# Weight loads queued behind a small transfer out of a gathered tile, and separate buffers for the copies of narrow tiles

## The chip, the cores and the metric

The kernel runs on one core of one Trainium2 chip. The metric is the device time of one execution in microseconds (us). The core has TensorE (PE in the profile), VectorE (DVE), ScalarE (ACT), GpSimd (POOL) and SyncE (SP), each with a queue of its own that it works through in order, and 16 DMA engines that all transfers share.

## The reference

```python
kv  = einsum('bhsd,bhse->bhde', k, v)           # batch 8, heads 8, seq 576, head_dim 64
a   = einsum('bhsd,bhde->bhse', q, kv)
a   = a / sqrt(mean(a*a, -1) + 1e-6) * g_norm
x   = a.transpose(0, 2, 1, 3).reshape(4608, 512)
e   = argmax(x @ w_gate); gate_w = softmax prob of e      # 8 experts
h   = relu(disp[e] @ w1[e])                      # 512 -> 1024
y   = h @ w2[e]                                  # 1024 -> 512
out = gate_w * y, back in token order (rows beyond an expert's capacity stay 0)
```

All inputs and outputs are float32.

## The kernel before, in words

The first part, up to about 166 us, computes the attention batch by batch, writes the rows (each with its normalization factor and gate) to a DRAM tensor `x_dram`, and builds a table that says which token stands in which slot of which expert. One expert, picked early, is the first; its first 384 rows (`EARLY`) are already under way in that part.

The second part goes through the eight experts in turn, with a fixed number of rows each (`BUDGET`: 704, 672, 640, 624, 592, 576, 560, 512), cut into tiles of 128 rows and a remainder. For an expert:

- **Rows.** GpSimd gathers a tile of rows from `x_dram` with an indirect DMA (`Rows.fetch`, line 439) into one of four buffers `xg`. VectorE or GpSimd multiplies by the normalization factor (`norm`, line 447). For the remaining rows 384 to 704 of the first expert (`rows`, line 1173; three tiles, of 128, 128 and 64 rows) TensorE transposes the result (line 459), and ScalarE and VectorE copy it into a high and a low float16 half `xs` (lines 677 and 467). For the other experts (`rows_beside`, line 1589) the two halves are made first and a DMA transpose on SP's queue turns them (line 482).
- **Weights.** SP loads `w1` and `w2` of the next expert in quarters of 512 KB into `raw1` and `raw2` (`load_weight`, line 327). VectorE takes the maximum of every eighth (line 343), one more instruction joins them (`a`, line 351), TensorE carries that across partitions (lines 356 and 363), VectorE makes a scale (lines 367 to 372), ScalarE writes the high half (line 377) and VectorE the low half (line 383). `weights` (line 1538) sets this up; its argument `after` names operations behind which the loads are planned. For the second expert that is the list `sent` that `rows` returns: the issues of the first expert's three gathers.
- **Products.** TensorE computes the first product in eight column blocks (line 531) into two PSUM buffers; ScalarE takes the high half of the rectified result (line 536), VectorE the low half (line 539). The second product (line 577) writes a PSUM bank per tile; ScalarE scales it into a buffer `ysb` (line 602) and GpSimd scatters it to `out` (line 607). A tile of at most 112 rows (`NARROW`; six experts have one) is computed the other way round (line 586); VectorE copies it to `yt` (`keep`, line 592), TensorE transposes it back (line 597), and then it goes to `ysb`. `yt` and `ysb` share one ring of three buffers.

The order on every engine is written by a planner (`Plan`, line 96) when the program is built: a list scheduler in which every operation has a duration, dependences, a key for its priority, and rings that model buffers. SP issues and DMA transfers are operations of it too ("S" and "D"). The order it finds is emitted engine by engine; on the chip the engines run through it and wait for one another by semaphores. A changed dependence or ring can therefore move other instructions in any engine's order.

Of the kernel before, what the change touches and what calls it, by code (L numbers as in the profile page):

```python
# [12 lines left out]
F32 = mybir.dt.float32  # L13
# [67 lines left out]
class Ring:  # L81
# [3 lines left out]
    def new(self):  # L85
        self.holds.append(Hold(self.holds[-self.n] if len(self.holds) >= self.n else None))
        return self.holds[-1]
# [8 lines left out]
class Plan:  # L96
# [5 lines left out]
    def op(self, ways, fn, deps=(), key=0.0, takes=(), uses=(), late=0.0):  # L102

        ways = [ways] if isinstance(ways[0], str) else list(ways)
        o = Op(ways, fn, [d for d in deps if d is not None], list(takes), key, late)
        for h in takes + uses if isinstance(takes, tuple) and isinstance(uses, tuple) else list(takes) + list(uses):
            h.users.append(o)
        self.ops.append(o)
        return o
# [56 lines left out]
def attention_moe_kernel(  # L166
# [12 lines left out]
    nc = tc.nc  # L179
    NB, H, S, D = q.shape  # L180
    N, DM = out.shape
    E = w_gate.shape[1]
    F = w1.shape[2]
    P = 128
# [67 lines left out]
    warm = cst.tile([1, 1], F32, name="warm")  # L252
# [21 lines left out]
    kv_bds = []  # L274
    for i in range(2):
        t = cst.tile([P, H, 2, XW], F32, name=f"kv_bd{i}")
        nc.gpsimd.memset(t, 0.0)
        kv_bds.append(t)


    mv_all = cst.tile([P, NT], F32, name="mv_all")
# [134 lines left out]
    def spans(s0, s1):  # L416

        cuts = [s0] + list(range((s0 // P + 1) * P, s1, P)) + [s1]
        return [(a, b - a, NHI if a % P else a // P) for a, b in zip(cuts, cuts[1:])]

    class Rows:


        def __init__(self, pool, gidx, s0, s1, size, bufs=3, rows=N, raw=None):
            self.pool, self.gidx, self.s0, self.bufs, self.rows, self.raw = pool, gidx, s0, bufs, rows, raw or pool
            self.tiles = spans(s0, s1)
            apart = "" if raw is None else f"_{s0}"
            self.xs = pool.tile([P, 2, KD, size], F16, name="xs" + apart)
            self.gt = pool.tile([P, NHI], F32, name="gt" + apart)
            self.xg, self.xm, self.pair = {}, {}, {}  # L430
# [122 lines left out]
    class Gemm2:  # L553
# [34 lines left out]

        def keep(self, i, yp):
            n = self.tiles[i][1]  # L590
            self.yt = self.pool.tile([P, DM], F32, tag="ysb", name="yt", bufs=self.bufs)
            nc.vector.tensor_copy(self.yt[:, 0:KD * n], yp[:, 0:KD * n])

        def turn(self, i, yp):
# [74 lines left out]
    op = plan.op  # L669
# [3 lines left out]
    new = lambda n: rings[n].new()  # L673

    def copy(e, out_, in_):
        if e == "A":
            nc.scalar.copy(out_, in_)
        else:
            nc.vector.tensor_copy(out_, in_)
# [41 lines left out]
    def kv_products(b, ts):  # L721
# [52 lines left out]

        o = op(("T", 0.31), turn, cut, key + 1, (a2,), (ks,))
        o = op([("A", 0.29), ("V", 0.34)], keep, [o], key + 1, (kt,), (a2,))
        o = op(("T", 0.42), gates, [o, ready], key + 1, (a3,), (kt,))
        done = [spread(u, f) for u in range(2) for f in range(2)]
# [12 lines left out]
    def unit(b, n, ts, kv, ready, oh):  # L791
# [18 lines left out]

        o = op(("T", 0.11 * m), turn, [qd], key - 1.2, (qp,), (qh,))
        kept = op([("A", 0.06 + 0.105 * m), ("V", 0.07 + 0.133 * m)], keep, [o], key - 1, (qt,), (qp,))
        done = []
        for w in range(2 if two else 1):
# [358 lines left out]
    def rows(gidx, s0, s1, n, slots_, key, low, pool, raw, bank, hold=None, size=None):  # L1173

        st, hold = {}, hold or Hold(None)
        fetched, gates, highs, lows = [], [], [], []
        landed = [w for ws in writes for w in ws]

        def fetch(e, i):
            if i == 0:  # L1180
                st["rows"] = Rows(pool, gidx()[0], s0, s1, size or s1 - s0, 3 if raw else 4, n, raw)
            st["rows"].fetch(i)

        for i in range(len(spans(s0, s1))):
            xg, xm, xp = new("xg"), new("xm"), new("x")
            o = op(("P", 1.05), lambda e, i=i: fetch(e, i), slots_ + landed + fetched[:1], key, (hold, xg))
            fetched.append(o)
            o = op(("D", 0.85), None, [o], key, (), (xg,))
            a = op([("V", 0.61), ("P", 1.05)], lambda e, i=i: st["rows"].norm(i, nc.vector if e == "V" else nc.gpsimd), [o],
                   low, (xm,), (xg,))  # L1190
            gates.append(op(("V", 0.07), lambda e, i=i: st["rows"].gate(i), [o], low, (), (xg, hold)))

            def turn(e, i=i, xp=xp):
                xp.t = bank()
                st["rows"].turn(i, xp.t)

            a = op(("T", 0.44), turn, [a], low, (xp,), (xm,))
            a = op([("A", 0.48), ("V", 0.61)],
                   lambda e, i=i, xp=xp: st["rows"].high(i, xp.t, lambda out_, in_: copy(e, out_, in_)), [a], low, (),
                   (xp, hold))  # L1200
            highs.append(a)
            lows.append(op(("V", 0.61), lambda e, i=i, xp=xp: st["rows"].low(i, xp.t), [a], low, (), (xp, hold)))
        return st, hold, fetched, (gates, highs, lows)

    def second(r, st, hh, hl, w2, scaled, hid, w_hold, sl_hold, s0, s1, bank, tiles=range(NHI), key=None):

        key = KEY * r if key is None else key
        urgent = key - KEY
        for i, (_, m, _) in enumerate(spans(s0, s1)):
            if i not in tiles:  # L1210
                continue
            yp, o = new(bank[0]), None
            k = key + 5 + 0.1 * i
            if m > NARROW:
                for c in range(0, 3 * KF, 4):

                    def product(e, i=i, c=c, yp=yp):
                        if c == 0:
                            yp.t = bank[1]()
                        st["g2"].products(i, yp.t, c, c + 4)  # L1220

                    js = range(c % KF, c % KF + 4)
                    after = [(hl if c >= 2 * KF else hh)[j] for j in js] + [scaled, o]
                    after += [w2[KF <= c < 2 * KF][j] for j in js] if w2 else []
                    o = op(("T", 0.86), product, after, k, (yp,), (hid, w_hold))
            else:
                yt = new("ysb")

                def product(e, i=i, yp=yp):
                    yp.t = bank[1]()  # L1230
                    st["g2"].turned_products(i, yp.t)

                o = op(("T", m / 25 + (0.25 if m > 50 else 0.5 if m > 40 else 1.1)), product, hh + hl + [scaled] + [x[j] for x in w2 or () for j in range(KF)], k, (yp,),
                       (hid, w_hold))
                o = op(("V", 0.07 + 4 * m / 960), lambda e, i=i, yp=yp: st["g2"].keep(i, yp.t), [o], urgent, (yt,), (yp,))
                yp = new(bank[0])

                def turn(e, i=i, yp=yp):
                    yp.t = bank[1]()
                    st["g2"].turn(i, yp.t)  # L1240

                o = op(("T", 0.4), turn, [o], key + KEY + 0.05, (yp,), (yt,))
            yh = new("ysb")

            def out_(e, i=i, yp=yp, yh=yh):
                yh.t = st["g2"].out(i, yp.t)

            o = op(("A", 0.58), out_, [o], urgent, (yh,), (yp,))
            o = op(("P", 1.05), lambda e, i=i, yh=yh: st["g2"].write(i, yh.t), [o], key, (), (yh, sl_hold))
            o = op(("D", 0.73), None, [o], key, (), (yh,))  # L1250
        return o
# [222 lines left out]
    def rest(last, n_i, e_tab, t_tab, keyc, zrow_i):  # L1474
        n_any = nc.values_load(n_i[0:1, 1:2], min_val=0, max_val=MAXT + 2)
        with tc.If(n_any > 0):
# [17 lines left out]
            with tc.For_i(0, n_t) as i:  # L1494
# [29 lines left out]
                for f in steps:  # L1524
# [3 lines left out]
    plan = Plan(plan.free)  # L1528
    op = plan.op
    rings.update({n: Ring(m) for n, m in (("h", 2), ("y", 2), ("x", 2), ("xs", 2), ("xg", 4), ("xm", 2), ("pair", 2),  # L1530
                                          ("ysb", 3), ("hid", 1), ("slots", 3))})
    for i in range(2):
        rings.update({f"w{i}_{s}": Ring(1) for s in range(2)} | {f"e{i}": Ring(2)})
        rings.update({f"raw{i}_{p}": Ring(1) for p in range(4)})
# [89 lines left out]
    def products(r, x, xh, xl, gates, xs_hold, si, sl_hold, sets, zs, w_holds, s0, s1):  # L1624
# [29 lines left out]
        def scales(e):  # L1654
# [3 lines left out]
        scaled = op(("V", 1.2), scales, hh[:1] + gates + [o for _, o, _ in zs], urgent, (),  # L1658
                    (xs_hold, *[x for _, _, x in zs]))
        o = second(r, st, hh, hl, sets and sets[1], scaled, hid, w_holds[1], sl_hold, s0, s1, y_bank)  # L1660
        if r == REST_AFTER:
            early["later"] = scaled
# [10 lines left out]
    o = op(("S", 0.01), moved, [early["scaled"]], -9 * KEY, (), tuple(ews))  # L1673
# [6 lines left out]
    for r in range(E):  # L1680
        products(r, *args)
        key = KEY * r
        if r + 1 < E:
            before = [] if r > 1 else sent
            st, xs_hold, sl, gates, turned, sent, asked = rows_beside(r + 1, key + ROWS)
# [3 lines left out]
        else:  # L1689
            steps, o = plan_rest(), early["later"]  # L1690
            for _ in range(68):
                o = op(("V", 0.2), lambda e: next(steps, None), [o], key + 1)
# [36 lines left out]
```

## Time and profile before

| | |
|---|---|
| median of 3 runs | 579.97 us (577.83 to 583.57) |
| the profiled execution's own time | 578.9 us |
| its span, first to last instruction | 577.1 us |
| mean granted TensorE clock | 0.968 of full speed |
| busy, share of the span | PE 91%, DVE 66%, ACT 43%, POOL 38% |
| HBM read and written | 73.13 MB and 20.61 MB |

Times in the rows count from the first instruction of the span. A row of the timeline says when a run of like instructions began, how long it took, how many it were, and in square brackets how long the engine had been idle before and what it waited for. The recorded ends of TensorE instructions are modelled; the starts are not.

### The profile page before, as it was taken

Reading aid. Unit: us, or ns where it says so; the run is one execution under the profiler, and the core shown is the slowest. Engines: PE = TensorE matmul, PEld = TensorE weight load, DVE = VectorE, ACT = ScalarE, POOL = GpSimd, SP = SyncE. Lnnn points to the kernel's source line nnn. Section 1 sums busy time; section 2 is a strip of 40 time slices with the busy share of each in tenths; the row PEclk is TensorE's granted clock in tenths of the full one; section 3 lists DMA queues with packets and bytes.
Section 4 is the critical chain, followed back from the end, with each engine's and each line's share of the span. In section 5 each row is a group of like instructions: output and inputs, shape, how many; then the busy total and the mean of one; then the engine's idle time right before and its main releaser. Section 6 shows DMA issues by size and latency. Waiting matters only on the chain.

```text
span 577.1 us, 12423 instructions
## 1 busy us (share of the span) xinstructions
PE 525.8 (91%) x4727; PEld 346.3 (60%) x4727; DVE 378.3 (66%) x1007; ACT 250.9 (43%) x496; POOL 218.1 (38%) x290
## 2 busy tenths in 40 slices
PE   4969697896997979998999999999999999999995
PEld 4868686683544646643774476477557648845442
DVE  4357679989976978999899186638629615721200
ACT  2737475875412536471825253362525445211210
POOL 3002332455334578556343632464263271011011
PEclk9979899986998999999999999999999999999998
DMA  8997999744249659595965572756365251011001
GB/s 277 374 347 242 352 370 378 233 160 154 94 134 351 152 139 336 110 314 186 222 224 155 132 196 78 218 111 225 113 163 195 77 100 50 2 37 38 0 31 38
DMA packets 78021, 102.61 MB, mean 178 GB/s; under 512 B 43222, under 2 KB 51414, under 8 KB 76932
## 3 DMA queue, kind: packets, MB, share of 16 engines
q1 hardware_dynamic: 69600, 70.43, 41.5%
q0 software_dynamic: 7776, 31.30, 15.6%
q8 instruction: 39, 0.64, 0.5%
q14 instruction: 26, 0.21, 0.1%
q10 hardware_dynamic: 580, 0.02, 0.1%
HBM read 73.13 MB, written 20.61 MB: 162 GB/s over the span
## 4 chain that ended last, share of the span: by engine, by line
PE 25%; issue 15%; DMA 5%; DVE 2%; POOL 2%; ACT 1%; POOLq 0%; DVEq 0%; ACTq 0%
PE yp L577 12%; PE hp L531 12%; DMA out_dram<-ysb,si 5%; PE yp L586 1%; DVE w2l L383 1%; POOL xg L439 1%; DVE hl L539 1%; POOL xm L447 0%; ACT w1h L377 0%; ACT w2h L377 0%; POOLq L1664 0%; POOL pair L477 0%; POOL out_dram L607 0%; PE pt_max L356 0%; PE pt_max L363 0%
## 5 line engine op out<-in xcount | busy, mean ns | idle before, releaser
L531 PE MATMUL hp<-xs,w1h 128*128 128x320 f16 (+6 forms) x896 | 134.1, 301 | 0.4 <-DVE hl L539 0.3
L531 PEld LDWEIGHTS <-w1h 128*128 128x128 f16 x960 | 94.0, 99 | 43.2 <-issue 5.9
L607 POOL DMA_INDIRECT out_dram<-ysb,si x41 | 43.0, 1048 | 143.0 <-ACT ysb L602 108.6
L577 PEld LDWEIGHTS <-hh 128*128 128x128 f16 x560 | 54.5, 98 | 65.4 <-issue 2.3
L536 ACT ACTIVATE hh<-hp 128x320 f16<-128x320 f32 (+7 forms) x64 | 40.8, 637 | 110.8 <-PE hp L531 108.2
L343 DVE TENSOR_REDUCE am<-raw 128x1 f32<-128x512 f32 x120 | 75.5, 675 | 4.3 <-DMA raw<-in_moe_w_dram 4.2
L531 PE MATMUL hp<-xs,w1l 128*128 128x320 f16 (+6 forms) x448 | 71.5, 300 | 0.0
L477 POOL TENSOR_TENSOR pair<-xm,pair 128x512 f16<-128x512 f32 (+5 forms) x35 | 45.1, 1290 | 64.8 <-ACT pair L473 60.0
L539 DVE SCALAR_TENSOR_TENSOR hl<-hp,hh 128x320 f16<-128x320 f32 (+7 forms) x64 | 47.3, 738 | 33.8 <-ACT hh L536 33.6
L577 PE MATMUL yp<-w2h,hl 128*128 128x512 f16 x272 | 65.9, 386 | 0.0
L602 ACT ACTIVATE ysb<-yp,ysc 128x512 f32<-128x512 f32 (+5 forms) x40 | 27.3, 683 | 88.0 <-PE yp L577 80.2
L577 PE MATMUL yp<-w2h,hh 128*128 128x512 f16 x272 | 64.4, 379 | 0.8 <-ACT ysb L602 0.8
L577 PE MATMUL yp<-w2l,hh 128*128 128x512 f16 x272 | 64.6, 379 | 0.0
L531 PEld LDWEIGHTS <-w1l 128*128 128x128 f16 x480 | 46.6, 98 | 19.3 <-issue 0.4
L439 POOL DMA_INDIRECT xg<-x_dram,gi x41 | 41.7, 1017 | 38.4 <-DVE gi L641 24.5
L383 DVE SCALAR_TENSOR_TENSOR w2l<-raw,sw,w2h 128x512 f16<-128x512 f32 x64 | 48.1, 797 | 10.7 <-ACT w2h L377 10.7
L823 PE MATMUL op<-kv_bd,qt 128*128 128x144 f32 x256 | 44.5, 319 | 7.5 <-issue 2.9
L383 DVE SCALAR_TENSOR_TENSOR w1l<-raw,sg,w1h 128x512 f16<-128x512 f32 x64 | 47.1, 789 | 0.9 <-ACT w1h L377 0.8
L577 PEld LDWEIGHTS <-hl 128*128 128x128 f16 x280 | 27.3, 99 | 32.8 <-issue 1.6
L823 PEld LDWEIGHTS op<-kv_bd,qt 128*128 128x128 f32 x256 | 38.3, 213 | 10.6 <-issue 4.3
L377 ACT ACTIVATE w1h<-raw,sg 128x512 f16<-128x512 f32 x62 | 39.7, 712 | 7.0 <-DVE sg L372 7.0
L377 ACT ACTIVATE w2h<-raw,sw 128x512 f16<-128x512 f32 x62 | 39.8, 710 | 5.3 <-PE yp L586 2.9
(257 smaller groups left out, 702.2 us busy)
## 6 DMA issues: line engine op xcount, KB each, us to landing
raw<-in_moe_w_dram SPq DMA_DIRECT2D x64, 512.0 KB
k_sb<-in_k_dram SPq DMA_DIRECT2D x16, 576.0 KB
v_sb<-in_v_dram SPq DMA_DIRECT2D x16, 576.0 KB
x_dram<-o_sb POOLq DMA_DIRECT2D x8, 1152.0 KB
q_sb<-in_q_dram SPq DMA_DIRECT2D x16, 512.0 KB
x_dram<-o_sb POOLq DMA_DIRECT2D x8, 144.0 KB
q_sb<-in_q_dram SPq DMA_DIRECT2D x32, 32.0 KB
xg<-x_dram,gi POOLq DMA_INDIRECT x41
```

The lines of the kernel that those rows point to most:

```text
L343: nc.vector.tensor_reduce(out=am()[:, p:p + 1], in_=raw[:, sl(p)], axis=AX.X, op=ALU.max, apply_absolute_value=True)
L377: nc.scalar.activation(wh[:, sl(p)], raw[:, sl(p)], AF.Copy, scale=z["s"])
L383: nc.vector.scalar_tensor_tensor(out=wl[:, sl(p)], in0=raw[:, sl(p)], scalar=z["s"], in1=wh[:, sl(p)], op0=ALU.mult, op1=ALU.subtract)
L439: nc.gpsimd.indirect_dma_start(out=self.xg[i][0:n], out_offset=None, in_=x_dram[0:self.rows, :], in_offset=bass.IndirectOffsetOnAxis(ap=se ...
L477: nc.gpsimd.tensor_tensor(out=pair[0:n, 1], in0=self.xm[i][0:n], in1=pair[0:n, 0], op=ALU.subtract)
L531: nc.tensor.matmul(self.view(hp)[:, u], lhsT=w[:, c, j * P:(j + 1) * P], rhs=x[:, c, u * hw:(u + 1) * hw], start=(t == 0 and c == 0), stop ...
L536: nc.scalar.activation(self.out(self.hh, j), self.view(hp), AF.Relu)
L539: nc.vector.scalar_tensor_tensor(out=self.out(self.hl, j), in0=self.view(hp), scalar=0.0, in1=self.out(self.hh, j), op0=ALU.max, op1=ALU.s ...
L577: nc.tensor.matmul(yp[0:n, 0:DM], lhsT=h[:, j, o:o + n], rhs=w[:, j, :], start=(m == 0), stop=(m == len(self.terms) - 1))
L602: nc.scalar.activation(self.ysb[0:n], yp[0:n, 0:DM], AF.Copy, scale=self.ysc[0:n, i:i + 1])
L607: nc.gpsimd.indirect_dma_start(out=out[:, :], out_offset=bass.IndirectOffsetOnAxis(ap=self.sidx[0:n, col:col + 1], axis=0), in_=ysb[0:n], ...
L823: nc.tensor.matmul(y, lhsT=qt.t[:, i * P:(i + 1) * P], rhs=kv2[:, half * HH + i], start=True, stop=True)
```

## The change

Three things. In `rows`, when it is called for rows that do not begin at 0 (the remaining rows of the first expert), one more SP operation is planned after the third gather has landed: a transfer of one float from that gathered tile to the one-element tile `warm`. It is appended to the list that `rows` returns, so all eight loads of the second expert's weights are planned behind it; on SP's queue they stand behind an instruction that waits for the gather. The tile's buffer `xg` counts as used by that transfer. Second, `yt` is no longer taken from the ring `ysb`: two views of `kv_bds`, tiles of the attention part, are used in turn. Third, the planner has a ring `yt` of two for them.

```diff
@@ after the two tiles kv_bd0 and kv_bd1 are made
+    yts = [t.rearrange("p h f x -> p (h f x)")[:, 0:DM] for t in kv_bds]
@@ Gemm2.keep
-            self.yt = self.pool.tile([P, DM], F32, tag="ysb", name="yt", bufs=self.bufs)
+            yts.append(yts.pop(0))
+            self.yt = yts[0]
             nc.vector.tensor_copy(self.yt[:, 0:KD * n], yp[:, 0:KD * n])
@@ rows
             o = op(("D", 0.85), None, [o], key, (), (xg,))
+            if s0 and i == len(spans(s0, s1)) - 1:
+                fetched.append(op(("S", 0.3), lambda e, i=i: nc.sync.dma_start(warm[0:1, 0:1], st["rows"].xg[i][0:1, 0:1]),
+                                  [o], key, (), (xg,)))
@@ second, the narrow tile
-                yt = new("ysb")
+                yt = new("yt")
@@ rings
-                                          ("ysb", 3), ("hid", 1), ("slots", 3))})
+                                          ("ysb", 3), ("yt", 2), ("hid", 1), ("slots", 3))})
```

## Rows read from the trace of the kernel before

**Rows 1.** Busy time by stretch: PE, PEld, DVE, ACT, POOL; granted clock, DMA share, GB/s

```profile
176.00:181.20 5.20, 1.88 (x13) 1.10 (x13) 2.82 (x10) 0.58 (x1) 2.43 (x4) 1.00 0.97 340
181.20:184.60 3.40, 3.40 (x11) 1.24 (x10) 3.40 (x7) 0.37 (x1) 0.77 (x1) 0.51 1.02 392
184.60:211.20 26.60, 26.60 (x244) 17.03 (x242) 24.60 (x49) 13.53 (x25) 16.79 (x19) 1.00 0.63 158
211.20:216.70 5.50, 1.30 (x11) 0.64 (x6) 1.12 (x3) 0.00 (x0) 3.57 (x4) 0.88 0.70 203
...
266.00:282.00 16.00, 12.70 (x156) 8.00 (x155) 14.77 (x30) 8.20 (x14) 9.72 (x12) 1.00 0.60 139
282.00:577.00 295.00, 287.46 (x2049) 175.47 (x2047) 153.59 (x356) 105.47 (x169) 96.28 (x106) 0.99 0.41 114
```

**Rows 2.** Timeline of TensorE, 172 to 195 us: start, length, instruction [idle before]

```profile
174.48 0.60 PE L459 MATMUL xp<-ident,xm 128*128 128x128 f32 x4
174.92 1.03 PE L577 MATMUL yp<-w2l,hh 128*128 128x512 f16 x4
176.73 0.66 PE L459 MATMUL xp<-ident,xm 128*128 128x128 f32 x4 [0.79 <-issue]
...
180.84 0.43 PE L459 MATMUL xp<-ident,xm 64*128 64x64 f32 x4 [2.58 <-DVE gt L454]
181.20 3.54 PE L577 MATMUL yp<-w2h,hl 128*128 128x512 f16 x8
184.53 1.34 PE L531 MATMUL hp<-xs,w1h 128*128 128x320 f16 x8
...
194.40 0.27 PE L356 MATMUL pt_max<-ident,a 128*1 128x128 f32 x1
```

**Rows 3.** Timeline of VectorE, 173 to 191 us

```profile
173.20 0.69 DVE L447 TENSOR_TENSOR xm<-xg 128x512 f32<-128x512 f32 x1 [2.02 <-issue]
...
175.98 0.69 DVE L447 TENSOR_TENSOR xm<-xg 128x512 f32<-128x512 f32 x1 [1.63 <-DMA xg<-x_dram,gi]
...
179.41 0.68 DVE L447 TENSOR_TENSOR xm<-xg 64x512 f32<-64x512 f32 x1 [2.36 <-DMA xg<-x_dram,gi]
...
181.42 0.67 DVE L343 TENSOR_REDUCE am<-raw 128x1 f32<-128x512 f32 x1
...
182.34 3.04 DVE L343 TENSOR_REDUCE am<-raw 128x1 f32<-128x512 f32 x5
...
190.59 0.68 DVE L343 TENSOR_REDUCE am<-raw 128x1 f32<-128x512 f32 x1
```

**Rows 4.** Timeline of GpSimd, 169 to 182 us

```profile
169.35 1.03 POOL L439 DMA_INDIRECT xg<-x_dram,gi  x1 [0.48 <-issue]
170.69 0.95 POOL L439 DMA_INDIRECT xg<-x_dram,gi  x1 [0.30 <-DMA out_dram<-ysb,si]
171.95 0.92 POOL L439 DMA_INDIRECT xg<-x_dram,gi  x1 [0.30 <-issue]
...
175.37 0.97 POOL L439 DMA_INDIRECT xg<-x_dram,gi  x1 [0.30 <-issue]
...
181.02 0.95 POOL L439 DMA_INDIRECT xg<-x_dram,gi  x1 [2.16 <-DVE si L641]
```

**Rows 5.** Timeline of SP's queue, 160 to 200 us: transfers issued

```profile
172.14 4.38 SPq L327 DMA_DIRECT2D raw<-in_moe_w_dram  x6
191.92 1.37 SPq L482 DMA_TRANSPOSE xs<-pair  x1
193.51 0.40 SPq L327 DMA_DIRECT2D raw<-in_moe_w_dram  x1
```

**Rows 6.** The tile `yt`: its copies, and what VectorE sat idle for before them

```profile
L592 DVE COPY yt<-yp x6: 283/424/625, 215.0 to 528.3; 128x256 f32<-128x256 f32 x2, 128x128 f32<-128x128 f32 x1, 128x448 f32<-128x448 f32 x1, 128x320 f32<-128x320 f32 x1
...
  PE yp L586: 43.9, 3
...
  DVE yt L592: 4.2, 1
```

## The prediction, made before the changed kernel ran

> **What bounds the kernel now.** I read the table by stretch first [rows 1]. From 282 us to the end TensorE is busy 287.46 of 295.00 us: there the experts run at TensorE's pace, and no wait elsewhere can be taken out of the time. What a changed order can win lies before 282, in the stretches where TensorE's busy time is short of the stretch. There are three: 176.0 to 181.2 (1.88 of 5.20), 211.2 to 216.7 (1.30 of 5.50), 266 to 282 (12.70 of 16.00, so 3.3 idle). Between the first two TensorE is full (26.60 of 26.60) and VectorE nearly so (24.60).
>
> The change acts in the first, so I opened that one engine by engine. TensorE waits 0.79 us and 2.58 us before the transposes of the second and the third tile of the first expert's remaining rows [rows 2]. Then the eight matmuls at 181.20 take 3.33 us to the next start, where four of the kind at 174.92 took 1.03; the granted clock of that stretch is 0.51, its lower level of 1.2 GHz, after 3.3 us of idle in the stretch before [rows 1]. So this place costs 0.79 + 2.58 + half of 3.33 (1.67) = 5.0 us. VectorE says what came last: it stood idle 1.63 and 2.36 us for the gathered tiles themselves [rows 3]. GpSimd issued the three gathers at 169.35, 170.69 and 171.95 [rows 4]; their first readers start at 173.20, 175.98 and 179.41, that is 3.85, 5.29 and 7.46 us after the issue, though the third has only 64 rows. What lies between the first and the others is SP: six loads of 512 KB, issued from 172.14 on [rows 5]. So the last gathers stand in competition with weights that nobody reads before 181.42 [rows 3].
>
> **The change part by part.**
>
> *Removed: the weight loads beside the gathers.* If the third gather takes what the first took, 3.85 us, its reader starts at 175.80 instead of 179.41, 3.6 earlier; the second at 174.54, 1.4 earlier. TensorE's third block of transposes would stand at 180.84 - 0.79 - 2.58 = 177.47, and the multiplied tile is there by then: today it follows the start on VectorE by 1.43 us (179.41 to 180.84), which makes 177.2. Both idle times then go, and with them what the clock fell after. Upper end of the gain 5.0 us. Lower end 0: the gather might be late from something else. The upper end is nearer, because the first gather, alone, has its row; I take 5.0.
>
> By the Trainium skill, "DMA: Bandwidth & Descriptors", section "Queues, rings and completion order", each DMA engine takes turns between the queues that have work, a packet at a time; a gather beside loads would by that lose about as long as its own bytes take, and the sum would be close to no change. The rival that follows from it is below; the 7.46 us against 3.85 speak for more than that [rows 3, 4].
>
> *Added: the wait and the transfer on SP's queue.* SP reaches the loads at 172.14 now. It would stand until 175.80, issue the small transfer (nearest row 0.40 us for one load [rows 5]; bounds 0 and 0.73, a sixth of 4.38) and need about 0.7 to the first load: 176.9, so loads are 4.8 us later. Queued behind it on SP are the six loads (4.38 us, to about 181.3), and then a DMA transpose at 191.92; even moved forward by 5 us that has 5 us left, so SP delays nothing but the loads.
>
> *Who waits for the loads.* VectorE's maxima. Six run from 181.42 to 185.38 with no idle between (the one at 181.42, five from 182.34 [rows 3]), so three quarters had landed by their turn. Four quarters are 2.1 MB, at the 340 to 392 GB/s of those stretches 5.4 to 6.2 us [rows 1]: issued from 176.9, the last would land near 183, hardly later than VectorE now comes to it, but VectorE is free some 3.4 us sooner and would wait for the first. TensorE needs the joined maximum at line 356, now at 194.40 [rows 2]; the last maximum ends at 191.27 [rows 3]. With TensorE 5.0 earlier, at 189.4, the maximum must come 1.9 earlier than now or TensorE waits. Loss between 0 (loads land as fast as the stretch allows) and 5.0 (maxima of late quarters stand ahead of VectorE's halves of the first product, and TensorE, with two PSUM buffers, stops behind them). I take 0.7, near the lower end, since the gathers no longer share the DMA engines with the loads.
>
> *The buffer of the third tile.* Its next gather is the one at 181.02, and it must now also wait for the small transfer. The trace has no such transfer; bounded by 0 and by a whole gather (3.85), it lands by 179.7. The gather could be due at 177.6, so GpSimd may stand 2.1 us. GpSimd is busy 2.43 of 5.20 and 0.77 of 3.40 there [rows 1], and the gather stands fourth for its expert: 0.
>
> *`yt` in buffers of its own.* If the shared ring cost anything, the idle time before the six copies would be put to a transfer to `out`. It is put to TensorE's products (43.9 us in three) [rows 6]: VectorE waits for the data, not for the buffer. The pause from 211.2 to 216.7 is of that kind too, for the copy starts at 215.0, and I let it move along whole. On the chip 0.
>
> *The new order.* The planner works with the longer chain and the other ring and may place any engine's instructions otherwise. The trace shows no size for that. Bounds: the 3.3 us idle of 266 to 282, once gained and once lost. I take 0.
>
> Sum: -5.0 + 0.7 = -4.3 us. Between 184.6 and 282 VectorE, ScalarE, GpSimd and SP work on what TensorE delivers and would follow it forward; after 282 TensorE is the bound and a start that is 4.3 earlier is an end that is 4.3 earlier. The profiled execution took 578.9 (span 577.1 and 1.8 around it): 574.6. The runs' median is 1.1 higher, 579.97, which makes 575.7 there; I say **575**.
>
> **Rivals.**
>
> *More: the pauses later shrink too.* With weights and rows planned in another order, the 3.3 us of 266 to 282 go as well: 578.9 - 4.3 - 3.3 = 571.3, on the median's scale some 572.4; I put 571.5. For it: these are waits of TensorE's queue for other engines, the kind an order decides. Against: the change does not touch that place.
>
> *The change does not do what it says: gathers and loads take turns.* Then without the loads the second and third gather are earlier only by their own time on the engines: 128 and 64 rows of 576 floats, 0.29 and 0.15 MB, at 340 GB/s 0.87 + 0.43 = 1.3 us. TensorE still idles about 2 us before the third tile, the clock still falls, and the 0.7 stays: -0.6, 578.3, on the median's scale 579.4. The same time comes out if the maxima wait out the whole gain of 5.0. For it: the second gather's 5.29 is only 1.4 over the first. Against: the third's 7.46. I put 579.
>
> *Slower: the second expert's weights become the bound.* Loads 4.8 later, none of it recovered: the joined maximum is ready at 191.27 + 4.8 = 196.1, 1.7 after TensorE's line 356 stands there today, the gain of 5.0 is lost, and what TensorE then waits for is behind on everything that follows from the scale: high halves, low halves, the release of `raw1`, the third expert's loads, and the stretch 266 to 282, whose 3.3 us come a second time. 1.7 + 3.3 = 5.0: 583.9, on the median's scale 585; with part of it covered by the pause at 211.2, 583. It decides from the point at which the maximum comes later than 194.40. For it: VectorE has 2.0 us to spare between 184.6 and 211.2 [rows 1]. Against: the loads have the DMA engines to themselves.
>
> **How the numbers follow.** Forecast 0.42, more 0.18, no gain 0.25, slower 0.15. Some 1% (5.8 us) is what a measurement of this kernel can tell from no change. Faster by more than that means under 574.2: most of the second case and a quarter of the forecast's, whose own range is 572 to 578: 0.26. Slower by more means over 585.8: nearly half of the last case, 0.08. Within: 0.66. The range from 570.5 to 582 holds the forecast with the bounds of its loss, the no-gain case and most of the case of more; left out are most of the slower case and the far end of the gain.
>
> **What would show it.** Right: SP's first load of `w1` behind 175 us; the reader of the third tile on VectorE at about 175.8; the first matmul of line 531 at 179.5 to 180.5 instead of 184.53, and no stretch at 0.51 before it; every later landmark of TensorE (line 356 at 194.40, the copy to `yt` at 215.0) earlier by about the same. Wrong in the size: line 356 or the first PSUM blocks with idle that names VectorE's maxima, and there idle for the DMA of `raw`. Wrong in the cause: the third gather still some 7 us from issue to reader with no load in flight. For the second rival up: less idle at 266 to 282. If `yt` matters on the chip, the pause before line 597 changes while the lines before it do not.

## The result, and the profile after

The changed kernel takes 587.53 us in the median of 6 runs (584.80 to 589.13), the kernel before 579.93 (6 runs beside it). The ratio is 1.0146, 95% interval 1.011 to 1.0183: slower by some 8 us, outside the range that was forecast. The profiled execution of after has a span of 585.7 us, before 577.1: 8.6 us to explain. In the changed kernel every line number is one or two higher than before (531 is 532, 482 is 483); e6, e7 and e11 shift it further (531 is 539), and so do e9 and e12 (531 is 542).

The gathers first. GpSimd's timeline after (start, length, instruction, [idle before]):

```profile
168.08 1.03 POOL L440 DMA_INDIRECT xg<-x_dram,gi  x1 [0.48 <-issue]
169.41 0.95 POOL L440 DMA_INDIRECT xg<-x_dram,gi  x1 [0.30 <-DMA out_dram<-ysb,si]
170.68 0.91 POOL L440 DMA_INDIRECT xg<-x_dram,gi  x1 [0.30 <-issue]
...
174.10 1.14 POOL L440 DMA_INDIRECT xg<-x_dram,gi  x1 [0.30 <-issue]
...
178.05 0.95 POOL L440 DMA_INDIRECT xg<-x_dram,gi  x1 [0.30 <-issue]
...
212.99 2.81 POOL L478 TENSOR_TENSOR pair<-xm,pair 32x512 f16<-32x512 f32 x1
...
285.28 1.08 POOL L609 DMA_INDIRECT out_dram<-ysb,si  x1 [3.85 <-ACT w2h L378]
291.70 1.10 POOL L609 DMA_INDIRECT out_dram<-ysb,si  x1 [5.34 <-DMA out_dram<-ysb,si]
```

SP's queue after:

```profile
174.82 0.23 SPq L1192 DMA_DIRECT2D warm<-xg  x1
177.07 5.28 SPq L328 DMA_DIRECT2D raw<-in_moe_w_dram  x6
...
194.88 22.12 SPq L483 DMA_TRANSPOSE xs<-pair  x5
```

VectorE after:

```profile
171.96 0.69 DVE L448 TENSOR_TENSOR xm<-xg 128x512 f32<-128x512 f32 x1 [2.05 <-issue]
...
173.70 0.69 DVE L448 TENSOR_TENSOR xm<-xg 128x512 f32<-128x512 f32 x1 [0.59 <-DMA xg<-x_dram,gi]
...
174.72 0.68 DVE L448 TENSOR_TENSOR xm<-xg 64x512 f32<-64x512 f32 x1
...
182.55 1.28 DVE L344 TENSOR_REDUCE am<-raw 128x1 f32<-128x512 f32 x2 [3.13 <-DMA raw<-in_moe_w_dram]
186.02 1.28 DVE L344 TENSOR_REDUCE am<-raw 128x1 f32<-128x512 f32 x2 [2.19 <-DMA raw<-in_moe_w_dram]
...
187.81 0.49 DVE L540 SCALAR_TENSOR_TENSOR hl<-hp,hh 128x320 f16<-128x320 f32 x1
...
291.93 0.16 DVE L643 COPY gi<-gidx_tab 128x6 int32 x1
296.47 0.17 DVE L643 COPY si<-sidx_tab 128x6 int32 x1 [4.38 <-issue]
```

The change does what it says: the third gather, issued at 170.68, is read at 174.72, 4.04 us later, against 7.46 [rows 3, 4]; the first load follows the small transfer. But the first pair of maxima of `w1` waits until 182.55 and the next pair until 186.02, and the first low half of the first product (`hl`) stands behind them on VectorE's queue, at 187.81. Before, these maxima did not wait [rows 3]. TensorE after:

```profile
176.15 0.43 PE L460 MATMUL xp<-ident,xm 64*128 64x64 f32 x4 [0.17 <-DVE xs L468]
...
179.01 1.25 PE L532 MATMUL hp<-xs,w1h 128*128 128x320 f16 x8 [0.60 <-ACT xs L679]
...
188.35 2.29 PE L532 MATMUL hp<-xs,w1h 128*128 128x320 f16 x8 [5.92 <-DVE p2t L309]
...
199.73 0.27 PE L357 MATMUL pt_max<-ident,a 128*1 128x128 f32 x1
...
219.87 4.36 PE L532 MATMUL hp<-xs,w1h 128*128 128x336 f16 x15 [3.86 <-DMA xs<-pair]
...
299.20 3.38 PE L532 MATMUL hp<-xs,w1h 128*128 128x320 f16 x16 [3.59 <-DVE hl L540]
```

The idle of 2.58 us [rows 2] is 0.17 now, and the first product starts at 179.01 instead of 184.53. Then come three long stops: 5.92, 3.86 and 3.59 us. (For the first the profile names `p2t`, a short instruction right behind that `hl`; it is the `hl` that reads the PSUM buffer which line 532 writes next.) The kernel before has none at the first and the third place. Near the second it has one of its own, 4.20 us ahead of line 597 at 215.62; in after that one is 1.51 (at 215.27), so the second stop takes its place in part. The table by stretch of after shows them (columns as in [rows 1]):

```profile
179.00:188.30 9.30, 3.42 (x24) 2.34 (x24) 3.98 (x8) 1.49 (x3) 1.22 (x2) 0.97 1.01 374
...
215.30:219.90 4.60, 0.74 (x6) 0.45 (x7) 3.20 (x8) 4.00 (x7) 3.50 (x5) 0.84 0.46 113
219.90:250.30 30.40, 30.40 (x195) 19.88 (x196) 26.59 (x54) 14.26 (x23) 16.30 (x19) 0.91 0.72 222
...
288.90:300.00 11.10, 7.48 (x54) 5.27 (x54) 6.51 (x17) 1.49 (x3) 6.53 (x7) 1.00 0.95 337
300.00:585.70 285.70, 278.34 (x1972) 168.56 (x1969) 143.93 (x330) 97.65 (x156) 88.74 (x100) 0.99 0.35 99
```

In the first, VectorE is busy 3.98 of 9.30 us while the DMA engines are full (1.01, 374 GB/s): they carry the weights VectorE waits for, and not those alone: GpSimd's queue (the gathers of the second expert's rows, issued from 174.10 to 178.05, and a scatter) takes 29.3% of the DMA engines' time there, SP's 71.9%. Behind a stop the next matmuls are slow as well: fifteen take 4.36 us at 219.87, where sixteen of the kind take 2.44 at 225.75; the granted clock from 219.90 to 224.00 is 0.50, the lower level of 1.2 GHz. From 300 on TensorE is busy 278.34 of 285.70, as before.

Different executions reach this part at times up to 5 us apart, which the part ahead of it decides. So all kernels are set side by side from the start of the stage, the first matmul of line 577 into `yp` (before: 167.58), all read from TensorE's timeline. Columns: that start; then, counted from it, the first matmul of the first expert's remaining first product, of its second product, and of the second products of the second and the third expert.

| kernel | start | first product | second product | expert 2 | expert 3 |
|---|---|---|---|---|---|
| before | 167.58 | 16.95 | 30.40 | 77.84 | 137.99 |
| after | 166.31 | 12.70 | 33.53 | 84.02 | 148.03 |
| e1 wait only | 167.52 | 11.73 | 35.16 | 84.78 | 151.50 |
| e2 `yt` only | 168.92 | 16.41 | 30.44 | 78.13 | 138.24 |
| e3 wait, old order | 166.29 | 11.74 | 32.74 | 81.42 | 141.82 |
| e4 new order, no wait | 167.63 | 16.01 | 30.23 | 80.82 | 146.24 |
| e5 four slots | 167.83 | 11.72 | 32.05 | 81.56 | 139.95 |
| e6 maxima behind | 167.07 | 11.73 | 27.09 | 77.28 | 142.27 |
| e7 both | 164.16 | 11.72 | 27.05 | 77.30 | 136.25 |
| e8 plan told | 168.07 | 11.73 | 27.04 | 78.17 | 145.36 |
| e9 last tile early | 168.09 | 11.73 | 27.13 | 83.03 | 144.14 |
| e10 before, four slots | 166.30 | 17.07 | 30.43 | 77.32 | 137.49 |
| e11 both, no wait | 168.50 | 16.73 | 31.82 | 81.81 | 141.79 |
| e12 scatter behind | 169.23 | 11.73 | 26.80 | 76.86 | 135.94 |

The profile of e9 is of an execution well above that kernel's median (584.81 against 579.38), so its row is not compared, and a stop read in it need not be in the others.

The 8.6 us of after against before are then: start 1.27 earlier (not the change's), first product 4.25 earlier, first product longer by 7.38 (20.83 against 13.45), second expert longer by 3.05 (50.49 against 47.44), third longer by 3.86 (64.01 against 60.15), and 0.2 less in the rest.

### The profile page after: what moved, and what is told of

Read it like the earlier page. It is cut to its first block, busy times and chain, and to the rows that moved or that the text cites. A ratio compares the mean times of both kernels' runs of the same rounds, so it can differ in the third digit from the quotient of the medians.

```text
span 585.7 us, 12417 instructions
## 1 busy us (share of the span) xinstructions
PE 527.3 (90%) x4727; PEld 345.5 (59%) x4727; DVE 379.1 (65%) x1008; ACT 251.5 (43%) x496; POOL 218.6 (37%) x289
## 4 chain that ended last, share of the span: by engine, by line
PE 43%; issue 21%; DMA 13%; DVE 13%; POOL 6%; ACT 2%; SPq 1%; POOLq 0%; DVEq 0%; ACTq 0%
PE hp L532 17%; PE yp L578 13%; DMA out_dram<-ysb,si 9%; PE op L825 3%; DVE ss L858 2%; PE qp L807 2%; DVE w2l L384 2%; POOL xg L440 2%; PE yp L587 2%; POOL pair L478 1%; PE a L737 1%; DMA v_sb<-in_v_dram 1%; POOL xm L448 1%; DMA raw<-in_moe_w_dram 1%; DVE hl L540 1%
## 5 line engine op out<-in xcount | busy, mean ns | idle before, releaser
L532 PE MATMUL hp<-xs,w1h 128*128 128x320 f16 (+6 forms) x896 | 137.4, 306 | 14.7 <-DVE p2t L309 6.7
L532 PE MATMUL hp<-xs,w1l 128*128 128x320 f16 (+6 forms) x448 | 73.1, 304 | 0.0
L478 POOL TENSOR_TENSOR pair<-xm,pair 128x512 f16<-128x512 f32 (+5 forms) x35 | 43.9, 1255 | 76.2 <-ACT pair L474 75.9
L578 PE MATMUL yp<-w2h,hl 128*128 128x512 f16 x272 | 64.4, 379 | 0.0
L384 DVE SCALAR_TENSOR_TENSOR w1l<-raw,sg,w1h 128x512 f16<-128x512 f32 x64 | 51.8, 857 | 1.3 <-ACT w1h L378 1.3
L384 DVE SCALAR_TENSOR_TENSOR w2l<-raw,sw,w2h 128x512 f16<-128x512 f32 x64 | 46.9, 783 | 8.6 <-ACT w2h L378 8.6
```

Of the source, the lines that this page charges most:

```text
L384: nc.vector.scalar_tensor_tensor(out=wl[:, sl(p)], in0=raw[:, sl(p)], scalar=z["s"], in1=wh[:, sl(p)], op0=ALU.mult, op1=ALU.subtract)
L478: nc.gpsimd.tensor_tensor(out=pair[0:n, 1], in0=self.xm[i][0:n], in1=pair[0:n, 0], op=ALU.subtract)
L532: nc.tensor.matmul(self.view(hp)[:, u], lhsT=w[:, c, j * P:(j + 1) * P], rhs=x[:, c, u * hw:(u + 1) * hw], start=(t == 0 and c == 0), stop ...
L578: nc.tensor.matmul(yp[0:n, 0:DM], lhsT=h[:, j, o:o + n], rhs=w[:, j, :], start=(m == 0), stop=(m == len(self.terms) - 1))
```

## The experiments

**Taking the change apart.** Theories: A, the late loads stand in VectorE's queue; B, the planner's new order costs, the wait itself helps; C, the buffers of `yt` cost.

*e1, the small transfer and its entry in the plan alone:* before plus the three lines of the change in `rows`. Expected:

> The kernel before with the small transfer, its wait and its place in the plan alone; `yt` stays in the ring of `ysb`. Theories: (A) the loads that land late stand in VectorE's queue, as maxima, ahead of the second halves of the first product, and that is paid wherever the chip waits; (B) the wait itself helps by some 4 us, and what costs is the other order that the planner makes when it is told of the wait; (C) the buffers of `yt` cost. A and B: 585 to 589, as the whole change. C: 575 to 580. In the trace by A: idle of VectorE for the DMA of `raw` near 182 and 186, and TensorE waiting for the joined maximum or the halves near 188.

590.49 us, ratio 1.0198 (1.0111 to 1.0285), a little above the 585 to 589 of A and B. C is out: without the new `yt` it is no faster.

*e2, the buffers of `yt` alone:* after without those three lines. Expected:

> The changed kernel without the small transfer and its entry in the plan: the buffers of `yt` alone. A (late loads in VectorE's queue) and B (the plan told of the wait) both say 578 to 582, as before; C (the buffers of `yt` cost): about 587. The pause of TensorE ahead of the copies of narrow tiles near 211 to 216 as in the kernel before by A and B; shorter if the ring mattered.

579.45 us, ratio 1.001 (0.9974 to 1.0047): no change, as forecast for this part. The pause near 211 to 216, though, is 0.69 us here, and "shorter" was to speak for the ring; the section on the prediction comes back to it.

*e3, the wait on the chip, the order of before:*

```diff
 def load(e, i, p, regs):
+    if r == 1 and i == 0 and p == 0:
+        nc.sync.dma_start(warm[0:1, 0:1], early["left"]["rows"].xg[2][0:1, 0:1])
```

> The kernel before with its plan and its order of instructions on every engine unchanged, and the small transfer put into SP's queue ahead of the first load of the second expert's `w1`: the wait on the chip without the planner knowing of it. A (late loads in VectorE's queue): VectorE meets six maxima in a row whose loads are some 5 us later than in the kernel before, ahead of the second halves of the first product: 582 to 588. B (the wait helps, the planner's new order costs): about 575.

580.74 us, ratio 1.0032 (0.9987 to 1.0076): neither. The first product starts 5.2 us earlier from the stage's start, and the second 2.3 later. TensorE's timeline of e3:

```profile
182.87 1.23 PE L531 MATMUL hp<-xs,w1h 128*128 128x320 f16 x4 [4.13 <-DVE xs L467]
...
232.03 4.11 PE L531 MATMUL hp<-xs,w1h 128*128 128x336 f16 x16 [3.73 <-DVE hl L539]
```

The stop of A is there in the old order too: the first maximum stands ahead even of the last half of `xs`. So in the old order the wait gains nothing, and most of what after loses is not the wait.

*e4, the new order without the wait:* after's plan; the small transfer's operation emits nothing.

> The changed kernel with its plan and so its order of instructions as it is, but with no small transfer on the chip: SP comes to the loads without waiting for the gather. A (late loads in VectorE's queue): 578 to 582, since the loads land about as early as in the kernel before and the gathers are slow again. B (the new order costs, with or without the wait): 584 to 588.

585.79 us, ratio 1.0116 (1.0021 to 1.0211): B. By the medians the order alone costs most of the 1.46%, though the loads run beside the gathers again. TensorE and then VectorE in e4:

```profile
217.96 4.36 PE L532 MATMUL hp<-xs,w1h 128*128 128x336 f16 x15 [3.92 <-DMA xs<-pair]
...
299.03 3.71 PE L532 MATMUL hp<-xs,w1h 128*128 128x320 f16 x16 [3.03 <-DVE hl L540]
```

```profile
291.66 0.17 DVE L643 COPY gi<-gidx_tab 128x6 int32 x1
296.31 0.17 DVE L643 COPY si<-sidx_tab 128x6 int32 x1 [4.48 <-issue]
```

These are after's second and third stop. Both theories hold, each for its own place: A for the first stop, B for the two others.

**Mending one stop at a time.**

*e5:* after, with four buffers instead of three for `gi` and `si`, the order untouched.

```diff
-            t = pool.tile([P, NHI + 1], I32, name=f"{nm}{s0}", bufs=3)
+            t = pool.tile([P, NHI + 1], I32, name=f"{nm}{s0}", bufs=4)
```

> The changed kernel with four buffers instead of three for the index tiles `gi` and `si` on the chip; the plan and every engine's order are as in the changed kernel. The third late stall (TensorE idle 3.59 us at 299.20, VectorE's copy into `si` idle 4.38 us before it) is put down to that copy waiting until the scatter that read the buffer has landed. If so: the copy has no idle time, the stall is gone with about 1 us of halved clock behind it, and the time is about 583 against 587.5. Rival: the copy stands for something else, or TensorE meets the next wait at once: 587.

581.13 us, ratio 1.0059 (1.0023 to 1.0095), against 1.0146 for after some 5 us better, more than expected. The third stop is gone, and with it the copy's idle time (VectorE of e5):

```profile
290.78 0.16 DVE L643 COPY gi<-gidx_tab 128x6 int32 x1
290.86 0.17 DVE L643 COPY si<-sidx_tab 128x6 int32 x1
```

So that copy had waited for the scatter that read the buffer. After's GpSimd rows above show why it was late: issued at 291.70, after 5.34 us behind the landing of the scatter of 285.28, beside six loads.

*e6:* after, VectorE's eight maxima of the second expert's `w1` moved in the finished order.

```diff
+            if r == 1 and i == 0:
+                hl = early["hl0"]
+                plan.moves = [(t, hl[k]) for t, k in zip(tops[::-1], (5, 5, 4, 4, 3, 3, 1, 1))]
```

The list goes through the maxima from the last to the first and counts the halves from 0: the first two maxima stand right behind the second half (`hl[1]`), the last two behind the sixth, and their join behind these.

> The changed kernel with its plan and order, but VectorE's eight maxima of the second expert's `w1` moved behind halves of the first product: two behind the second half, two behind the fourth, two behind the fifth, two behind the sixth. The wait on the chip stays. Theory: what the wait gained (TensorE at its first matmul of line 532 5.5 us earlier) was lost because these maxima, whose loads are late, stand ahead of the halves; then TensorE does not stop at 181.7 to 188.4, the second product starts near 192.5 instead of 199.84, and the time is 580 to 582. Rival: the gain is given back later in any case, since the second expert's rows (the DMA transposes at 219.87) bound TensorE: 585 to 588.

583.61 us, ratio 1.0103 (1.0059 to 1.0147). The second product starts 27.09 after the stage's start instead of 33.53; the second and the third stop remain (3.96 and 4.90 us in its profile). In the profiled execution 5.8 of the 6.4 us gained are still there at expert 3. The median shows less, 3.9 under after and above the expected 580 to 582, and the intervals of the two ratios overlap; so e6's time alone does not price the first stop. e7 against e5 does.

*e7, e5 and e6 together:*

> Both edits together: the maxima of the second expert's `w1` behind halves of the first product, and four buffers for `gi` and `si`. If each takes away a stall that lies on the path, the sum of both: 576 to 578, under the kernel before. If the second expert's rows at 219.87 give the first gain back: 582 to 584.

576.52 us, ratio 0.9943 (0.9894 to 0.9992): as expected, and faster than before, if only just clear of the noise. Against e5 (1.0059, from 1.0023), which differs by the place of the maxima alone, it is 1.2% faster. TensorE of e7, what is left:

```profile
181.62 1.25 PE L539 MATMUL hp<-xs,w1h 128*128 128x320 f16 x8 [0.69 <-DVE hl L547]
183.81 1.25 PE L539 MATMUL hp<-xs,w1h 128*128 128x320 f16 x8 [0.40 <-DVE hl L547]
187.84 1.25 PE L539 MATMUL hp<-xs,w1h 128*128 128x320 f16 x8 [0.62 <-DVE hl L547]
...
211.42 4.36 PE L539 MATMUL hp<-xs,w1h 128*128 128x336 f16 x15 [3.92 <-DMA xs<-pair]
```

*e8, the planner told:*

```diff
-                fetched.append(op(("S", 0.3), lambda e, i=i: nc.sync.dma_start(warm[0:1, 0:1], st["rows"].xg[i][0:1, 0:1]),
+                fetched.append(op(("S", 2.5), lambda e, i=i: nc.sync.dma_start(warm[0:1, 0:1], st["rows"].xg[i][0:1, 0:1]),
+            if r == 1 and i == 0:
+                loads = [op(("L", 0.01), None, [o], key, late=3.5) for o in loads]
```

> The changed kernel with the planner told more nearly what the chip showed: the small transfer holds SP's queue for 2.5 us in the plan instead of 0.3, and the data of the second expert's `w1` count as there 3.5 us after the plan's landing. Nothing else is edited, and the planner makes its own order, in which halves of the first product stand between the maxima. If the loss came from the plan's wrong landing times: no stop of TensorE between the first and the third block of line 532, and 576 to 582. If any new order costs some 7 us in the later stretches, as the run of the new order without the wait suggests may be so: 583 to 588.

588.29 us, ratio 1.0177 (1.0112 to 1.0241). The first product is as short as in e7 (15.31 us), so it was the planner's landing times that led to the first stop. But the order differs again later: TensorE stops 3.04 us at 228.51 and 4.67 at 297.86. The latter is after's third stop again: the copy into `si` has 5.46 us of idle time ahead of it, and e8 has three buffers. Better numbers for one place do not make the whole order better.

*e10, the kernel before with four buffers (e5's edit), a control:*

> The kernel before with four buffers for `gi` and `si` instead of three, nothing else. If the late stall at 299 belongs to the changed kernel's order alone (before, the copy into `si` at 292.26 has no idle time): no change, 577 to 580. Rival: the three buffers cost the kernel before as well, at some other expert, and the gain of the four was no part of the change's cost: 572 to 575.

578.58 us, ratio 0.9984 (0.9945 to 1.0024): no change. The third stop needs both, the new order and the three buffers.

*e11, e7 without the small transfer on the chip:* the price of the wait.

> The kernel with the maxima behind the halves and four index buffers (576.5 us), but without the small transfer on the chip: the loads run beside the gathers again. It prices the wait by itself in an order that no longer loses its gain. If the wait is worth what the first product shows (start of the second product 27.05 us after the stage's start with it, 30.23 in the new order without it): 3 us slower, 579 to 581. Rival: the gain came from the order and the buffers alone: 576 to 577.

582.24 us, ratio 1.0054 (1.0022 to 1.0086): slower than e7 beyond both intervals, and by more than the 3 us expected. At expert 3 in the table it is 5.5 us. TensorE of e11 waits for the third tile again:

```profile
182.21 0.43 PE L467 MATMUL xp<-ident,xm 64*128 64x64 f32 x4 [2.93 <-DVE gt L462]
```

Its first product begins 5.0 us later than e7's and is 0.9 longer than e4's (15.09 against 14.22), with the moved maxima in it, which were not late here. Without that 0.9 the wait is worth 4 to 5 us in this order.

**The second stop, tried twice.**

*e9:* e7, the second expert's last tile (32 rows) in buffers of its own and its steps on VectorE, ScalarE and GpSimd (multiplication, cast, second half) moved ahead.

```diff
+                n5, h5, l5 = early["chain", 5]
+                plan.moves += [(n5, o), (h5, early["chain", 4][1]), (l5, early["chain", 4][2])]
```

> The kernel with the maxima behind the halves and four index buffers (576.5 us), and one edit more: the second expert's last tile of rows (32 rows) gets buffers of its own for its multiplied rows and its pair, and its steps on VectorE, ScalarE and GpSimd are moved ahead (its multiplication behind the scale of `w1`, its cast and its second half right behind those of the tile before). If the stall at 211.42 (TensorE idle 3.92 us for that tile's DMA transpose, and a halved clock behind it) is paid to the end: the transpose lands some 4 us earlier and the time is 571 to 573. Rival: VectorE, full from there to 240, gives it back as waits for halves: 575 to 577.

579.38 us, ratio 0.9968 (0.993 to 1.0005); not better than e7, and outside both ranges. In the profiled execution the stop for the transpose is gone and another one stands later, TensorE first, then ScalarE:

```profile
227.48 4.64 PE L542 MATMUL hp<-xs,w1h 128*128 128x336 f16 x16 [6.12 <-DVE p2t L319]
```

```profile
225.29 0.62 ACT L484 CAST pair<-xm 128x512 f16<-128x512 f32 x1 [6.21 <-POOL xm L458]
```

*e12:* e9, the scatter that delayed those gathers moved behind the fourth of them.

```diff
+        if r == 2:
+            plan.moves.append((early["written", 0, 2], asked[3]))
```

> The kernel of the last tile early (579.4 us, ratio 0.997 to before) with one instruction moved on GpSimd: the scatter of the first expert's narrow tile, which in that run stood idle 5.00 us at 219.15 ahead of three gathers of the third expert, now follows the fourth of them. In that run those late gathers made ScalarE's cast of a pair wait 6.21 us ahead of its activations, and TensorE stood 6.12 us at 227.48. If that wait took back what the early tile had gained: no such stop, and 570 to 574. Rival: the full VectorE from 213 to 245 takes it back in any order: 576 to 580.

578.28 us, ratio 0.9958 (0.9927 to 0.999); within the rival's range. The stop of e9 is not in its profile. But the transpose is late once more (TensorE, then GpSimd of e12). Ahead of the tile's second half GpSimd took 4.44 us over a scatter, where the one of after at 285.28 takes 1.08; that this made it late is read from the order, not tested:

```profile
216.00 4.36 PE L542 MATMUL hp<-xs,w1h 128*128 128x336 f16 x15 [4.98 <-DMA xs<-kv_bd]
```

```profile
203.72 4.44 POOL L619 DMA_INDIRECT out_dram<-ysb,si  x1 [2.19 <-ACT ysb L614]
...
211.55 1.14 POOL L488 TENSOR_TENSOR kv_bd<-kv_bd,kv_bd 32x512 f16<-32x512 f32 x1
```

So neither run prices the second stop, and whether it can be had back stays open; e7 and e12, both under before, can't be told apart (the intervals overlap).

## Why the prediction was wrong

**Removed: the loads beside the gathers.** Right in mechanism and in size. The third gather took 4.04 us where 3.85 was assumed, the first product starts 4.25 us earlier from the stage's start (5.0 forecast; 5.2 in e1, e3 and e5 to e8), and in an order that keeps it the wait is worth 4 to 5 (e7 against e11). The Trainium skill, "DMA: Bandwidth & Descriptors", section "Queues, rings and completion order", has each engine take turns between queues by packets, from which a gather would, by the prediction's estimate, lose about its own bytes' time, 0.43 us for the third. The trace disagrees with that estimate: it got 3.4 us faster.

**Who waits for the loads: here the prediction failed.** It named the mechanism, with a bound of 5.0 ("maxima of late quarters stand ahead of VectorE's halves of the first product, and TensorE, with two PSUM buffers, stops behind them"), and then took 0.7 "near the lower end, since the gathers no longer share the DMA engines with the loads". Measured: 7.38 us of lengthening against before, beyond that bound and more than the whole gain.

The reason given for the lower end does not hold. The first expert's gathers are out of the loads' way, but the second expert's four, issued from 174.10 to 178.05, now run beside them: from the first load's issue (177.07) to 182.52, just ahead of the first maxima, GpSimd's queue takes 40.1% of the DMA engines' time and SP's 47.5%. (No run takes these gathers away, so their share in the delay is not shown.) The sum reckoned the last quarter's landing from the bytes of four quarters at the stretch's whole rate; it saw that VectorE would wait for the first quarter too, and gave that no price. The first pair of maxima could start only at 182.55, 5.5 us behind the first load's issue, and the second at 186.02. What counted was these first ones, since everything behind them on VectorE's queue waits. With those maxima moved, the loss is not there (e6, e7).

That the loads left SP at 177.07, with 176.9 forecast, is luck. From the stage's start they leave after 10.76 us, against 4.56 before, so they are 6.2 later and not 4.8: SP needs 2.25 us from the small transfer (174.82) to the first load, where 1.1 was reckoned, and the whole stage stands 1.27 earlier in this execution.

**The new order: the second failure.** The prediction took 0, with 3.3 us either way. e4 puts the order alone at 1.16% (0.21% to 2.11%), some 7 us; in its profile they are 3.15 at the second expert (50.59 against 47.44) and 5.27 at the third (65.42 against 60.15). From the stage's start, the second half of the last tile starts on GpSimd after 43.4 us in e4 (before: 41.2) and the last scatter of the second expert after 123.8 (118.6). Each has a reader with no slack: TensorE, and the copy into `si`. Why the planner places them so was not looked into. That "after 282 TensorE is the bound and a start that is 4.3 earlier is an end that is 4.3 earlier" was wrong in this direction: a stretch in which TensorE has no idle time to lose can still gain some, at 299.20.

**`yt`.** Right: 0 (e2, in the old order; in the new one e1 and after differ by it too, and their intervals overlap). The copies' idle time is put to the products for the most part, as before; after, the rows of the tile that holds it, `kv_bd`, where before stood [rows 6]:

```profile
L594 DVE COPY kv_bd<-yp x6: 279/414/625, 214.7 to 536.7; 128x256 f32<-128x256 f32 x2, 128x128 f32<-128x128 f32 x1, 128x448 f32<-128x448 f32 x1, 128x320 f32<-128x320 f32 x1
...
  PE yp L587: 51.2, 4
```

**The pause from 211.2 to 216.7** was let move along whole, as a wait of the copy for TensorE's products. The rows of before do not show that of this copy:

```profile
215.04 0.42 DVE L592 COPY yt<-yp 128x256 f32<-128x256 f32 x1 [3.43 <-remote]
...
215.62 1.03 PE L597 MATMUL yp<-ident,yt 128*64 128x128 f32 x4 [4.20 <-DVE yt L592]
```

TensorE's last products of line 586 start at 210.91, and "remote" means that the profile finds no instruction that released the copy. So its cause stays open. The ring is not shown to be it: the pause is 0.69 us in e2, with buffers of its own, but as short (0.69 and 0.68) in e3 and e10, which keep the shared ring. Nor was it a fixed feature: those three, with the order of before, stop later instead, e2 for 3.20 us at 231.70, e3 for 3.73 at 232.03, e10 for 3.05 at 229.05 (the last section shows what stood there in e3 and e10). One profiled execution had shown one of two places for about the same loss.

**The rivals.** "No gain" (0.25) describes e3, the wait in the old order: 580.74, by the mechanism that it gives second ("the maxima wait out the whole gain"); its first one, gathers and loads in turns, is refuted by the 4.04 us. "Slower" (0.15) came out on its side and by its test, the joined maximum later than 194.40 (199.73, line 357), but its chain went wrong behind that point: TensorE stopped earlier, for the halves, and the later stops came with e4's order, not with the late loads. Its 583 is 4.5 short.

**The sum.** It ends at 575.7 on the median's scale, and 575 was said; that does not matter here. For the third tile's buffer 0 was right: the fourth gather goes at 178.05 after 0.30 us.

## What to carry to other kernels

A load that is sent later costs where its first reader stands in an in-order queue, not where its last reader ends: look at what is queued behind the first reader, and move that reader along with the load. Ask also which other transfers will run beside the load at its new time. When an order comes from a planner, one new dependence is a new order for the whole program; run the new order without the wait and the wait in the old order before either is believed. Stops that such an order brings in can hang on a ring one buffer short: e5 took away some 5 us with one number.

## What the runs showed that was not expected

In two traces an instruction of VectorE takes over 6 us while GpSimd works without a gap. VectorE of e10, the four-buffer kernel with the order of before:

```profile
220.89 6.75 DVE L383 SCALAR_TENSOR_TENSOR w2l<-raw,sw,w2h 128x512 f16<-128x512 f32 x2
```

Two instructions of 0.74 us (the median of their line) take 6.75, one of them 6.08 by its record, from 220.89 to 226.98. In e3 one takes 6.29, from 223.67 to 229.96, and GpSimd's timeline of e3 is without a gap there; the first of the two copies in the last row ends at 230.00:

```profile
223.88 1.07 POOL L447 TENSOR_TENSOR xm<-xg 128x512 f32<-128x512 f32 x1
224.92 1.17 POOL L477 TENSOR_TENSOR pair<-xm,pair 128x512 f16<-128x512 f32 x1
226.04 0.19 POOL L454 COPY gt<-xg 128x1 f32<-128x1 f32 x1
226.19 1.15 POOL L477 TENSOR_TENSOR pair<-xm,pair 128x512 f16<-128x512 f32 x1
227.32 2.09 POOL L447 TENSOR_TENSOR xm<-xg 128x512 f32<-128x512 f32 x2
229.38 1.28 POOL L454 COPY gt<-xg 128x1 f32<-128x1 f32 x2
```

The stop of 3.73 us at 232.03 in e3 comes right behind it, as does the one of 3.05 in e10: the next `hl`, which TensorE waits for, stands behind these two instructions on VectorE's queue. The maxima, with one input, stay at 662 to 687 ns all through after. The Trainium skill, "SBUF — State Buffer", section "Who interferes with whom", says that a VectorE instruction with two SBUF inputs contends with a GpSimd instruction that reads SBUF, and that the first to issue holds the shared pair of ports while the other blocks; the traces agree on the forms, but if this is that block, it lasted over seven GpSimd instructions in a row, not one. No run here takes those GpSimd instructions away, so this rests on the coincidence in time.
